# Loads issued earlier, exponentials ahead of the choice, score rows moved: a change of order in an attention and mixture-of-depths kernel

## The chip, the cores and the metric

One core of a Trainium2 chip runs the kernel. The metric is the device time of one execution in microseconds, as the median of the runs shown. The core has a matrix engine (TensorE, PE, whose weight loads are listed as PEld), a vector engine (VectorE, DVE), a scalar engine (ScalarE, ACT), GpSimd (POOL) and a sync engine (SyncE, SP), which here only issues DMAs. The engines run side by side; each one runs its own instructions in program order and waits on semaphores for the others.

## The reference

Efficient attention on 8 batches of 8 heads, 576 tokens and a head size of 64, followed by a mixture-of-depths block that sends 128 tokens of each batch through an MLP:

```python
q_s = softmax(q, axis=-1); k_s = softmax(k, axis=2)          # float32
kv = np.einsum('bhsd,bhse->bhde', k_s, v)
x = np.einsum('bhsd,bhde->bhse', q_s, kv)                    # to (B, S, H*D), H*D = 512
scores = np.einsum('bsd,d->bs', x, w_gate)
out = x.copy()
for b in range(B):
    top_idx = np.argpartition(-scores[b], capacity)[:capacity]     # capacity = 128
    xe = x[b, top_idx]
    ye = np.maximum(xe @ w1, 0.0) @ w2                             # 512 -> 1024 -> 512
    g = 1.0 / (1.0 + np.exp(-scores[b, top_idx]))
    out[b, top_idx] = xe + g[:, None] * ye
```

## The kernel before

A unit is one batch with four of its eight heads (`NU` = 16 units; unit u is batch u // 2, and `qd` = u % 2 says which four heads). Its 576 tokens are 512 main tokens, four to a partition, and 64 last ones; the last tokens of q, k and v are loaded for all eight heads at once with the unit whose `qd` is 0. `load(u, ...)` issues these loads on the sync queue: 0.52 MB for each of q, k and v, and 0.13 MB for each set of last rows, in pieces of 256 bytes. The pool `ld` has three buffers for each of q, k and v, so load(u) waits until unit u - 3 has been used up.

For each unit `prepare(u)` takes the exponentials of q and k on ACT (`q_exp`, `k_exp`; with `qd` = 0 those of the last rows too) and copies v on DVE next to a column of ones (`v_copy`). `kv_mm` makes the product of k's exponentials and v on PE, and `kv_out` turns it into a block-diagonal right-hand side (`kv_diag`) on ACT and DVE. `q_t` transposes q's exponentials on PE and scales them on the way out on ACT; `q_t_last` does the same for the last tokens, with DVE. `x_mm` makes the attention output in PSUM, `x_out` normalizes it on DVE and stores it with a DMA on the sync queue (0.52 MB per unit, and 0.13 MB for a batch's last tokens).

After the second unit of a batch `score` sums the gate scores on DVE, `score_last` folds the last tokens' scores with a small matmul (L325), and `score_row` transposes the scores to a row on PE, copied out by ACT. `compare` (DVE) compares every score with every other, `count` (PE, L370, copied out by ACT) adds the results to ranks, and `pick` (DVE, then ACT and POOL) finds the tokens with the chosen ranks: its gate is `g`, an ACT instruction, and it gathers the chosen rows from the output in DRAM with an indirect DMA on POOL (L388), which so needs the stores of that batch. `turn` transposes the gathered rows on PE (L404), `mlp1` and `mlp2` are the two MLP products in eight pieces each (L418, L428), and `finish` adds the result and scatters it back with POOL.

The order is written out by hand (`tc.manual_schedule()`): every engine, and the sync queue, gets its instructions in the order of the program text. One pass of the loop is a slot s. In slot s PE does kv_mm and the transposes of unit s + 1 and x_mm of unit s, while exponentials and copies are prepared for unit s + 2. In even slots from 2 on the batch (s - 2) // 2 is chosen (`compare`, `count`, `pick`); in odd slots the batch s // 2 gets its scores. From slot 4 on (`LAG`) the MLP of batch (s - 4) // 2 runs between these steps, mlp1 in the even slot and mlp2 in the odd one; `pieces(n)` puts n of the eight pieces there. `turn` stands at the head of the even slot.

Before the change prepare(s + 2) stands behind `pick`, and load(s + 3) at the end of the slot, behind the stores of x_out. The weights w1 and w2 (2.10 MB each) are loaded at the end of slots 0 and 1.

Of the kernel before, what the change touches and what calls it, by code (L numbers as in the profile page):

```python
# [8 lines left out]
F32 = mybir.dt.float32  # L9
# [8 lines left out]
def kernel(  # L18
# [20 lines left out]
    nc = tc.nc  # L39
    B, H, S, D = q.shape  # L40
    DM, F = moe_w1.shape
    P = 128
    R = 4
    MAIN = R * P
    REM = S - MAIN
    KD = DM // P
    KF = F // P
    SD = S * D
# [1 line left out]
    C = D + 2  # L50
    NG = 18
    LOW = 2.0 ** -30
    WARM = 12
    assert S == MAIN + 64 and D == 64 and DM == H * D and DM == 512 and H % 4 == 0
    assert 1 < capacity < S and KF == 8 and NQ == 2
    HALF = S // 2
# [5 lines left out]
    const = ctx.enter_context(tc.tile_pool(name="const", bufs=1))  # L62
    ld = ctx.enter_context(tc.tile_pool(name="ld", bufs=3))
# [6 lines left out]
    def bank(tag, bufs):  # L70
        return ps.tile([P, 512], F32, tag=tag, name=tag, bufs=bufs)

    def part(i):
        return slice(64 * i, 64 * i + 64)

    units = [(b, qd) for b in range(B) for qd in range(NQ)]
    NU = len(units)
# [3 lines left out]
    raw = {}  # L81

    def load(u, which):
        b, qd = units[u]
        for what in which:
            src = {"q": q, "k": k, "v": v}[what]
            t = ld.tile([P, 4, R, D], F32, tag=what, name=what)
            nc.sync.dma_start(  # L88
                out=t.rearrange("p h r d -> p h (r d)"),
                in_=bass.AP(tensor=src.tensor, offset=src[b, 4 * qd].offset,  # L90
                            ap=[[R * D, P], [SD, 4], [1, R * D]]))
            raw[what, u] = t
            if qd == 0:
                t = ld.tile([REM, H, D], F32, tag=what + "_l", name=what + "_l", bufs=2)
                nc.sync.dma_start(
                    out=t, in_=bass.AP(tensor=src.tensor, offset=src[b, 0].offset + MAIN * D,
                                       ap=[[D, REM], [SD, H], [1, D]]))
                raw[what + "l", b] = t

    load(0, "qkv")  # L100
    load(1, "qkv")
# [3 lines left out]
    ones_b = const.tile([P, 4 * P], BF16, name="ones_b")  # L105
    nc.vector.memset(ones_b, 1.0)
    warm = const.tile([P, 1], F32, name="warm")
    nc.scalar.activation(out=warm, in_=ones_b[:, :1], func=AF.Exp)
    for _ in range(2):
        w_ps = bank("tp", 2)  # L110
        for _ in range(WARM // 2):
            nc.tensor.matmul(out=w_ps, lhsT=ones_b[:, :P], rhs=ones_b, start=True, stop=True)
    wgm = const.tile([P, NQ, 2, 2, D], F32, name="wgm")
    nc.sync.dma_start(out=wgm.rearrange("p a i h d -> p (a i h d)"),
                      in_=bass.AP(tensor=moe_w_gate.tensor, offset=moe_w_gate.offset,
                                  ap=[[0, P], [1, DM]]))
    w1 = const.tile([P, KD, F], F32, name="w1")
    w2 = const.tile([P, KF, DM], F32, name="w2")
# [7 lines left out]
    for n in range(2):  # L126
        t = const.tile([P, 4, R, D + 1], F32, name=f"v_ones{n}")
# [3 lines left out]
        t = const.tile([P, H, D + 1], F32, name=f"v_last{n}")  # L131
# [3 lines left out]
        t = const.tile([P, H, D], F32, name=f"k_last{n}")  # L135
        nc.gpsimd.memset(t[part(1)], 0.0)
        k_last.append(t)
        t = const.tile([P, 2, 2, C], F32, name=f"kv_diag{n}")
# [23 lines left out]
    def late_constants():  # L162
        nc.vector.tensor_add(fold, ident[:, :REM], ident[:, REM:])
        nc.vector.tensor_scalar(after, col_minus_p, 0.0, None, op0=OP.is_gt)
        for h in range(2):
            nc.vector.memset(wgm[part(h), :, :, 1 - h], 0.0)
# [8 lines left out]
    def k_exp(u):  # L175
        b, qd = units[u]
        ke = at.tile([P, 2, R, 2, D], F32, tag="ke", name="ke")
        kr = by_row(raw.pop(("k", u)))
        for i in range(2):
            nc.scalar.activation(out=ke[:, i], in_=kr[:, i], func=AF.Exp)  # L180
        st["ke", u] = ke
        if qd == 0:
            nc.scalar.activation(out=k_last[b % 2][part(0)], in_=raw.pop(("kl", b)), func=AF.Exp)

    def q_exp(u):
        b, qd = units[u]
        qe = at.tile([P, 2, R, 2, D], F32, tag="qe", name="qe")
        qr = by_row(raw.pop(("q", u)))
        for i in range(2):
            nc.scalar.activation(out=qe[:, i], in_=qr[:, i], func=AF.Exp)  # L190
        st["qe", u] = qe
        if qd == 0:
            ql = at.tile([REM, H, D], F32, tag="ql", name="ql")
            nc.scalar.activation(out=ql, in_=raw.pop(("ql", b)), func=AF.Exp)
            st["ql", b] = ql
# [116 lines left out]
    def score(b):  # L312
        s = md.tile([P, R + 2], F32, tag="s", name="s")
        a = md.tile([P, NG], F32, tag="s_a", name="s_a")
        nc.vector.tensor_add(a, sr[b][:, 0], sr[b][:, 1])
        a3 = a.rearrange("p (n m) -> p n m", n=3)
        nc.vector.reduce_sum(out=s[:, 0:3], in_=a3[:, :, 0:4], axis=AX.X)
        nc.vector.reduce_sum(out=s[:, 3:4], in_=a3[:, 1:3, 4:6], axis=AX.XY)
        nc.vector.reduce_sum(out=s[:, 5:6], in_=a3[:, 0, 4:6], axis=AX.X)
        st["s", b] = s  # L320

    def score_last(b):
        s = st["s", b]
        f_ps = bank("mm", 2)
        nc.tensor.matmul(out=f_ps[:REM, :1], lhsT=fold, rhs=s[:, 5:6], start=True, stop=True)  # L325
        nc.vector.tensor_copy(out=s[:REM, 4:5], in_=f_ps[:REM, :1])

    def score_row(b):
        s = st["s", b]
        srow = md.tile([P, S], F32, tag="srow", name="srow")  # L330
        t_ps = bank("tp", 2)
        for r in range(R):
            nc.tensor.transpose(out=t_ps[:, r * P:(r + 1) * P], in_=s[:, r:r + 1].to_broadcast([P, P]),  # L333
                                identity=ident)
        nc.scalar.copy(out=srow[:, :MAIN], in_=t_ps)  # L335
        l_ps = bank("tp", 2)
        nc.tensor.transpose(out=l_ps[:, :REM], in_=s[:REM, 4:5].to_broadcast([REM, P]),
                            identity=ident[:REM, :REM])
        nc.scalar.copy(out=srow[:, MAIN:], in_=l_ps[:, :REM])
        st["srow", b] = srow  # L340
# [183 lines left out]
    def prepare(u):  # L524
        q_exp(u)
        k_exp(u)
        v_copy(u)

    LAG = 4

    with tc.manual_schedule():
        prepare(0)
        late_constants()
        kv_mm(0)
        kv_out(0)
        q_t(0, 0)
        q_t(0, 1)
        q_t_last(0)
        load(2, "qkv")
        prepare(1)  # L540

        number = None
        for s in range(NU + LAG):

            mlp_b, odd = divmod(s - LAG, 2)
            busy = s >= LAG
            first = busy and odd == 0
            piece = mlp1 if first else mlp2
            f_next = 0

            def pieces(n):
                nonlocal f_next
                for _ in range(n if busy else 0):
                    each(piece, mlp_b, f_next)
                    f_next += 1

            ends = s // 2 if s % 2 == 1 and s < NU else None
            chosen = (s - 2) // 2 if s % 2 == 0 and 2 <= s <= NU else None
            if first:
                each(turn, mlp_b)  # L560
            if s + 1 < NU:
                kv_mm(s + 1)
                kv_out(s + 1)
                pieces(1)
                q_t(s + 1, 0)
                q_t(s + 1, 1)
            else:
                pieces(1)
            if s == NU - 1:
                x_mm(s)  # L570
                x_out(s)
                score(ends)
            if chosen is not None:
                compare(chosen)
            pieces(2)
            if s + 1 < NU:
                q_t_last(s + 1)
            if s < NU - 1:
                x_mm(s)
                x_out(s)  # L580
                if ends is not None:
                    score(ends)
            pieces(2)
            if chosen is not None:
                count(chosen)
                pick(chosen)
            if ends is not None:
                score_last(ends)
            if s + 2 < NU:
                prepare(s + 2)  # L590
            pieces(2)
            if ends is not None:
                score_row(ends)
            pieces(1)
            if busy and odd == 1:
                each(finish, mlp_b)
            if s == 0:
                nc.sync.dma_start(out=w1, in_=moe_w1.rearrange("(d p) f -> p d f", p=P))
            if s == 1:
                nc.sync.dma_start(out=w2, in_=moe_w2.rearrange("(f p) d -> p f d", p=P))  # L600
            if s + 3 < NU:
                load(s + 3, "qkv")
            if s == NU:
                number = sums_in_range()

# [27 lines left out]
```

## Time and profile before

| | us |
|---|---|
| median of 3 runs | 307.67 (307.02 to 307.70) |
| profiled execution, its own time | 306.83 |
| its span, first to last instruction | 305.0 |

| engine | busy us | share of the span | instructions |
|---|---|---|---|
| PE | 257.1 | 84% | 1669 |
| PE weight loads | 199.7 | 65% | 1669 |
| DVE | 120.8 | 40% | 452 |
| ACT | 99.4 | 33% | 210 |
| POOL | 21.0 | 7% | 32 |

The busy times come from one profiled execution. Weight loads overlap with matmuls. Each f32 matmul is recorded as two instructions. The mean granted clock of PE is 0.943 of 2.4 GHz; it changes between two levels in the course of the run. A row of the timeline gives the start, the busy time, the engine, the line, the operation with its tiles and, in brackets, how long the engine was idle before it and who released it.

### The profile page before, as it was taken

To read this page: it belongs to the slowest core of one execution; us is meant where nothing else is said; L and a number is where in the kernel's file an instruction comes from. 1 tells how busy PE (TensorE), PEld (TensorE's weight loads), DVE (VectorE), ACT (ScalarE), POOL (GpSimd) and SP (SyncE) were. 2 spreads that over 40 slices of the span, in tenths; PEclk is the share of its full clock that TensorE was granted. 3 is DMA by queue.
4 is the path that set the end of the run, shared out by engine and by line. 5 is a ranking of instruction groups with operands and counts; after the bars stand their busy time and mean duration, and the time that the engine had idled before them with its cause. 6 is when DMAs were issued, how large, how long until landed. Compare 5 with 4: busy or idle time off the path is not lost.

```text
span 305.0 us, 4416 instructions
## 1 busy us (share of the span) xinstructions
PE 257.1 (84%) x1669; PEld 199.7 (65%) x1669; DVE 120.8 (40%) x452; ACT 99.4 (33%) x210; POOL 21.0 (7%) x32
## 2 busy tenths in 40 slices
PE   6467737576997999799979998999979999998991
PEld 2456617475986588757967597749855887583850
DVE  1122332915463426332831465146524465351000
ACT  4256222245316331542265124703272411120100
POOL 5000000010001010101010001001010101101101
PEclk9679976959899999999999999999999999999997
DMA  7990799981946195808690586349552121201100
GB/s 186 296 262 12 243 373 378 218 273 65 234 134 224 38 236 145 276 0 220 161 290 21 168 213 204 108 100 256 148 189 72 50 69 34 89 34 37 38 6 37
DMA packets 51789, 46.77 MB, mean 153 GB/s; under 512 B 14256, under 2 KB 49072, under 8 KB 51760
## 3 DMA queue, kind: packets, MB, share of 16 engines
q1 hardware_dynamic: 50480, 42.21, 49.4%
q0 software_dynamic: 1280, 4.20, 3.9%
q8 instruction: 15, 0.25, 0.3%
q14 instruction: 14, 0.11, 0.1%
HBM read 34.87 MB, written 11.53 MB: 152 GB/s over the span
## 4 chain that ended last, share of the span: by engine, by line
PE 67%; DVE 11%; ACT 7%; DMA 6%; issue 3%; SPq 3%; POOL 0%; POOLq 0%; ACTq 0%
PE mm L428 16%; PE mm L418 14%; PE kv L212 11%; PE x L273 9%; PE tp L370 4%; DMA v<-in_v_dram 4%; PE tp L243 3%; PE kv L215 3%; DMA wgm<-in_moe_w_gate_dram 3%; DVE xs L292 3%; DVE junk_p L383 2%; SPq L88 2%; PE x L276 2%; ACT qe L190 2%; PE mm L404 1%
## 5 line engine op out<-in xcount | busy, mean ns | idle before, releaser
L418 PE MATMUL mm<-xT,w 128*128 128x128 f32 x512 | 63.1, 278 | 1.4 <-ACT xT L406 1.4
L212 PE MATMUL kv<-v_ones,ke 128*128 128x130 f32 x256 | 42.6, 318 | 25.3 <-ACT ke L180 14.0
L428 PE MATMUL mm<-w,hT 128*128 128x512 f32 x128 | 62.0, 608 | 0.0
L418 PEld LDWEIGHTS mm<-xT,w 128*128 128x128 f32 x512 | 59.2, 192 | 4.0 <-ACT xT L406 1.9
L212 PEld LDWEIGHTS kv<-v_ones,ke 128*128 128x128 f32 x256 | 38.6, 229 | 27.9 <-ACT ke L180 15.3
L428 PEld LDWEIGHTS mm<-w,hT 128*128 128x128 f32 x128 | 21.8, 189 | 17.4 <-issue 16.9
L273 PE MATMUL x<-kv_diag,qT 128*128 128x132 f32 x256 | 33.0, 282 | 0.0
L273 PEld LDWEIGHTS x<-kv_diag,qT 128*128 128x128 f32 x256 | 30.0, 190 | 1.5 <-issue 0.5
L227 ACT COPY kv_diag<-kv 64x130 f32<-64x130 f32 x32 | 8.4, 263 | 46.1 <-DVE krec L224 45.6
L421 ACT ACTIVATE hT<-mm 128x512 f32<-128x512 f32 x16 | 9.4, 590 | 39.9 <-PE mm L418 39.9
L245 ACT ACTIVATE qT<-tp,krec 128x512 f32<-128x512 f32 x32 | 20.3, 684 | 6.3 <-PE tp L243 6.2
L224 DVE RECIPROCAL krec<-kv 128x2 f32<-128x2 f32 x16 | 2.7, 170 | 48.9 <-PE kv L215 48.9
L436 DVE SCALAR_TENSOR_TENSOR o<-mm,g,xr 128x512 f32<-128x512 f32 x8 | 6.0, 750 | 39.2 <-PE mm L428 39.2
L190 ACT ACTIVATE qe<-q 128x512 f32<-128x512 f32 x32 | 18.3, 621 | 9.1 <-DMA q<-in_q_dram 9.1
L388 POOL DMA_INDIRECT xr<-out_dram,idx x8 | 9.0, 1131 | 161.9 <-PE mm L418 75.7
L335 ACT COPY srow<-tp 128x512 f32<-128x512 f32 x8 | 4.7, 584 | 44.8 <-PE tp L333 44.8
L180 ACT ACTIVATE ke<-k 128x512 f32<-128x512 f32 x32 | 18.2, 618 | 1.5 <-DMA k<-in_k_dram 1.5
L243 PEld LDWEIGHTS tp<-ident,qe 128*128 128x128 f32 x128 | 16.3, 152 | 2.6 <-issue 1.4
L243 PE MATMUL tp<-ident,qe 128*128 128x128 f32 x128 | 17.9, 286 | 0.0
L348 DVE TENSOR_SCALAR less<-srow,s 128x128 bf16<-128x128 f32 (+4 forms) x40 | 16.2, 405 | 0.0
L437 POOL DMA_INDIRECT out_dram<-o,idx x8 | 8.0, 1002 | 116.6 <-DVE o L436 106.1
L199 DVE COPY v_ones<-v 128x1024 f32<-128x1024 f32 x16 | 10.9, 680 | 13.0 <-DMA v<-in_v_dram 13.0
(80 smaller groups left out, 251.2 us busy)
## 6 DMA issues: line engine op xcount, KB each, us to landing
q<-in_q_dram SPq DMA_DIRECT2D x16, 512.0 KB
k<-in_k_dram SPq DMA_DIRECT2D x16, 512.0 KB
v<-in_v_dram SPq DMA_DIRECT2D x16, 512.0 KB
out_dram<-xs SPq DMA_DIRECT2D x16, 512.0 KB
w<-in_moe_w_dram SPq DMA_DIRECT2D x2, 2048.0 KB
q_l<-in_q_dram SPq DMA_DIRECT2D x8, 128.0 KB
k_l<-in_k_dram SPq DMA_DIRECT2D x8, 128.0 KB
v_l<-in_v_dram SPq DMA_DIRECT2D x8, 128.0 KB
```

The source lines that it names most:

```text
L180: nc.scalar.activation(out=ke[:, i], in_=kr[:, i], func=AF.Exp)
L190: nc.scalar.activation(out=qe[:, i], in_=qr[:, i], func=AF.Exp)
L199: nc.vector.tensor_copy(out=v_ones[u % 2][:, :, :, :D], in_=raw.pop(("v", u)))
L212: nc.tensor.matmul(out=kv[:, i], lhsT=ke[:, i, r].rearrange("p h d -> p (h d)"), rhs=vo[:, pair, r], start=(r == 0), stop=False)
L243: nc.tensor.transpose(out=t_ps[:, r * P:(r + 1) * P], in_=qe[:, i, r].rearrange("p h d -> p (h d)"), identity=ident)
L245: nc.scalar.activation(out=st["qT", u][:, i].rearrange("p r c -> p (r c)"), in_=t_ps, func=AF.Copy, scale=krec[:, u, i:i + 1])
L273: nc.tensor.matmul(out=x[:, r, i] if r < 3 else x[:, 1 + i, 2], lhsT=qT[:, i, r], rhs=kd[:, i], start=True, stop=True)
L348: nc.vector.tensor_scalar(less[rows, j, :cols.stop], srow[rows, :cols.stop], own, None, op0=OP.is_lt)
L370: nc.tensor.matmul(out=r_ps[:, a:z], lhsT=ones_b[rows, :P], rhs=rhs, start=(n == 0), stop=(n == len(todo) - 1), skip_group_check=True)
L418: nc.tensor.matmul(out=h_ps[:, f % 4 * m:(f % 4 + 1) * m], lhsT=w1[:, d, f * P:(f + 1) * P], rhs=xT[:, d, :m], start=(d == 0), stop=(d == ...
L421: nc.scalar.activation(out=hT[:, f - 3:f + 1, :m], in_=h_ps[:, :4 * m].rearrange("p (f c) -> p f c", f=4), func=AF.Relu)
L428: nc.tensor.matmul(out=st["y", b, n][:m], lhsT=st["hT", b, n][:, f, :m], rhs=w2[:, f], start=(f == 0), stop=(f == KF - 1))
```

## The change

The warm-up matmuls at the start get another form: 12 bf16 matmuls over 512 columns become 40 small f32 ones. `load` issues the last rows behind the main loads of all three tensors. load(2) and load(3) are issued behind prepare(0), w1 and load(4) behind prepare(1), and load(s + 5) in the slot, behind prepare(s + 2) and ahead of the stores of x_out; w2 in slot 0. prepare(s + 2) stands ahead of `compare`. In odd slots `score_last` stands two pieces later and `score_row` behind the eighth piece. In slot 15 x_mm stands at the head of the slot, ahead of all pieces.

```diff
@@ load
-            if qd == 0:
-                t = ld.tile([REM, H, D], F32, tag=what + "_l", name=what + "_l", bufs=2)
...
+        for what in which if qd == 0 else "":
+            src = {"q": q, "k": k, "v": v}[what]
+            t = ld.tile([REM, H, D], F32, tag=what + "_l", name=what + "_l", bufs=2)
...
@@ warm-up (WARM = 12 becomes 10)
-    for _ in range(2):
-        w_ps = bank("tp", 2)
-        for _ in range(WARM // 2):
-            nc.tensor.matmul(out=w_ps, lhsT=ones_b[:, :P], rhs=ones_b, start=True, stop=True)
+    ones_f = const.tile([P, P], F32, name="ones_f")
+    nc.vector.memset(ones_f, 1.0)
+    w_ps = [bank("tp", 2), bank("tp", 2)]
+    for n in range(2 * WARM):
+        c = part(n % 2)
+        nc.tensor.matmul(out=w_ps[0][c, 66 * (n // 2 % 4):66 * (n // 2 % 4) + 65], lhsT=ones_f[:, :64],
+                         rhs=ones_f[:, :65], start=True, stop=True)
+    for n in range(2 * WARM):
+        c = part(n % 2)
+        nc.tensor.matmul(out=w_ps[n % 2][:, 66 * (n // 2 % 4):66 * (n // 2 % 4) + 66], lhsT=ones_f[c],
+                         rhs=ones_f[c, :66], start=True, stop=True)
@@ ahead of the loop
+    def load_weights(n):
...
         prepare(0)
+        load(2, "qkv")
+        load(3, "qkv")
         late_constants()
...
         q_t_last(0)
-        load(2, "qkv")
         prepare(1)
+        load_weights(0)
+        load(4, "qkv")
@@ the slot
+            last = s == NU - 1
...
-            else:
+            elif not last:
                 pieces(1)
-            if s == NU - 1:
+            if last:
                 x_mm(s)
                 x_out(s)
                 score(ends)
+                pieces(3)
+                score_last(ends)
+                pieces(1)
+                score_row(ends)
+            if s + 2 < NU:
+                prepare(s + 2)
             if chosen is not None:
                 compare(chosen)
             pieces(2)
             if s + 1 < NU:
                 q_t_last(s + 1)
-            if s < NU - 1:
+            if s + 5 < NU:
+                load(s + 5, "qkv")
+            if s == 0:
+                load_weights(1)
+            if s < NU and not last:
                 x_mm(s)
                 x_out(s)
                 if ends is not None:
                     score(ends)
-            pieces(2)
+            if not last:
+                pieces(2)
             if chosen is not None:
                 count(chosen)
                 pick(chosen)
-            if ends is not None:
+            pieces(2)
+            if ends is not None and not last:
                 score_last(ends)
-            if s + 2 < NU:
-                prepare(s + 2)
-            pieces(2)
-            if ends is not None:
+                pieces(1)
                 score_row(ends)
-            pieces(1)
+            elif not last:
+                pieces(1)
             if busy and odd == 1:
                 each(finish, mlp_b)
-            if s == 0:
-                nc.sync.dma_start(out=w1, in_=moe_w1.rearrange("(d p) f -> p d f", p=P))
-            if s == 1:
-                nc.sync.dma_start(out=w2, in_=moe_w2.rearrange("(f p) d -> p f d", p=P))
-            if s + 3 < NU:
-                load(s + 3, "qkv")
```

## Rows read from the trace of the kernel before

**Rows 1.** The page's first part: busy us (share of the span) xinstructions of each engine.
```profile
PE 257.1 (84%) x1669; PEld 199.7 (65%) x1669; DVE 120.8 (40%) x452; ACT 99.4 (33%) x210; POOL 21.0 (7%) x32
```

**Rows 2.** Stretches: length, busy us of PE, PEld, DVE, ACT, POOL, PE clock, DMA share, GB/s.
```profile
75.39:94.28 18.89, 17.36 (x136) 15.94 (x135) 9.75 (x36) 6.72 (x16) 0.99 (x1) 0.91 0.80 215
94.28:126.45 32.17, 30.04 (x208) 23.31 (x208) 14.61 (x54) 12.14 (x27) 2.19 (x2) 1.00 0.59 165
```

**Rows 3.** Timeline of PE, slots 5 and 13: kv_mm and score_last with idle time before.
```profile
94.28 1.16 PE L212 MATMUL kv<-v_ones,ke 128*128 128x130 f32 x8 [1.53 <-ACT ke L180]
...
105.52 0.28 PE L325 MATMUL mm<-s,fold 128*64 128x1 f32 x2 [0.60 <-DVE s L319]
...
222.98 1.16 PE L212 MATMUL kv<-v_ones,ke 128*128 128x130 f32 x8 [1.53 <-ACT ke L180]
...
234.23 0.28 PE L325 MATMUL mm<-s,fold 128*64 128x1 f32 x2 [0.60 <-DVE s L319]
```

**Rows 4.** Timeline of ACT and DVE at the end of slot 6.
```profile
124.11 0.20 ACT L392 ACTIVATE g<-sel 128x1 f32<-128x1 f32 x1 [1.63 <-DVE junk_p L383]
124.22 1.13 ACT L190 ACTIVATE qe<-q 128x512 f32<-128x512 f32 x2
...
124.62 0.68 DVE L199 COPY v_ones<-v 128x1024 f32<-128x1024 f32 x1
...
125.21 0.41 DVE L201 COPY v_last<-v_l 64x512 f32<-64x512 f32 x1
...
125.78 1.13 ACT L180 ACTIVATE ke<-k 128x512 f32<-128x512 f32 x2
```

**Rows 5.** Timeline of slot 6: compare's last instruction, count's first, pick's first.
```profile
117.30 0.28 DVE L353 SCALAR_TENSOR_TENSOR ties<-srow,s,after 64x64 bf16<-64x64 f32 x1
...
120.08 0.29 PE L370 MATMUL tp<-less,ones_b 128*128 128x288 bf16 x1
...
122.52 0.82 DVE L383 SCALAR_TENSOR_TENSOR junk_p<-rank,slot_no,tok_row 128x576 bf16<-128x576 f32 x1 [2.33 <-ACT rank L372]
```

**Rows 6.** Timeline of PE in slot 5, behind x_mm.
```profile
102.56 0.45 PE L276 MATMUL x<-kv_diag,qTl 128*64 128x132 f32 x4
...
102.94 1.98 PE L428 MATMUL mm<-w,hT 128*128 128x512 f32 x4
```

**Rows 7.** Stretches ahead of slot 4; the last two columns are DMA share, GB/s.
```profile
2.00:23.50 21.50, 13.54 (x53) 9.81 (x52) 3.76 (x17) 7.55 (x16) 2.62 (x8) 0.78 1.07 267
23.50:32.00 8.50, 5.19 (x41) 4.51 (x40) 3.69 (x14) 4.90 (x10) 0.00 (x0) 0.96 0.01 3
32.00:68.00 36.00, 23.32 (x147) 20.72 (x148) 14.26 (x55) 10.80 (x24) 1.27 (x1) 0.77 1.03 314
```

**Rows 8.** The gather of batch 0 in POOL's timeline, and all gathers' times to landing.
```profile
60.78 1.27 POOL L388 DMA_INDIRECT xr<-out_dram,idx  x1 [55.98 <-DMA v_l<-in_v_dram]
...
DMA to landing us min/median/max: 3.3/4.6/6.9
```

**Rows 9.** Timeline of PE: kv_mm of units 2, 3 and 4.
```profile
32.04 1.13 PE L212 MATMUL kv<-v_ones,ke 128*128 128x130 f32 x8 [2.67 <-DVE v_ones L199]
...
46.81 2.07 PE L212 MATMUL kv<-v_ones,ke 128*128 128x130 f32 x8 [3.75 <-DVE v_ones L199]
...
62.79 2.10 PE L212 MATMUL kv<-v_ones,ke 128*128 128x130 f32 x8 [4.57 <-ACT ke L180]
```

**Rows 10.** Stretches at half clock: after kv_mm(4) starts, and in slot 4.
```profile
62.80:68.20 5.40, 5.40 (x25) 5.40 (x26) 0.17 (x1) 1.32 (x4) 0.00 (x0) 0.50 0.87 296
75.80:78.30 2.50, 2.50 (x14) 2.50 (x13) 0.00 (x0) 0.78 (x3) 0.00 (x0) 0.50 0.68 164
```

**Rows 11.** Timeline of the start: warm-up, kv_mm(0), and the mask of w_gate.
```profile
1.47 5.30 PE L112 MATMUL tp<-ones_b 128*128 128x512 bf16 x12 [1.47 <-DVE side L124]
...
11.68 2.07 PE L212 MATMUL kv<-v_ones,ke 128*128 128x130 f32 x8 [4.91 <-DVE v_ones L199]
...
16.84 0.64 DVE L166 MEMSET wgm<- 64x256 f32 x2 [4.44 <-DMA wgm<-in_moe_w_gate_dram]
```

More of the change, by code (lines that the diff above doesn't have):

```diff
@@ L52 @@
     LOW = 2.0 ** -30
-    WARM = 12
+    WARM = 10
     assert S == MAIN + 64 and D == 64 and DM == H * D and DM == 512 and H % 4 == 0
@@ L92, in load @@
             raw[what, u] = t
-            if qd == 0:
-                t = ld.tile([REM, H, D], F32, tag=what + "_l", name=what + "_l", bufs=2)
[L95 to L98, printed above, removed]
+        for what in which if qd == 0 else "":
+            src = {"q": q, "k": k, "v": v}[what]
+            t = ld.tile([REM, H, D], F32, tag=what + "_l", name=what + "_l", bufs=2)
+            nc.sync.dma_start(
+                out=t, in_=bass.AP(tensor=src.tensor, offset=src[b, 0].offset + MAIN * D,
+                                   ap=[[D, REM], [SD, H], [1, D]]))
+            raw[what + "l", b] = t
     load(0, "qkv")
@@ L529 @@
     LAG = 4
+    def load_weights(n):
+        if n == 0:
+            nc.sync.dma_start(out=w1, in_=moe_w1.rearrange("(d p) f -> p d f", p=P))
+        else:
+            nc.sync.dma_start(out=w2, in_=moe_w2.rearrange("(f p) d -> p f d", p=P))
     with tc.manual_schedule():
         prepare(0)
+        load(2, "qkv")
+        load(3, "qkv")
         late_constants()
```

## The prediction

> **What bounds the kernel now.** I read the busy shares first: TensorE (PE) is busy for 257.1 of 305.0 us, DVE, ACT and POOL for 40, 33 and 7% of the span [rows 1]. So the time is PE work plus PE's idle time, and the question is where the 48 us of idle lie. The table by stretches comes next. From slot 5 on the kernel repeats with a period of two slots: kv_mm(6) starts at 94.28 and kv_mm(14) at 222.98, four pairs later [rows 3], so a pair takes 128.70 / 4 = 32.18 us. PE is busy for 30.04 of them at full clock [rows 2]; 2.13 us are idle. The timeline of PE names them: 1.53 us ahead of kv_mm in each odd slot, released by the exponentials of k, and 0.60 us ahead of the little matmul of score_last, released by DVE [rows 3]. There are five of each, at 94.28 to 222.98 and at 105.52 to 234.23. The rest of the idle time lies ahead of 75.39 us, where slot 4 begins with turn(0), and in the tail. Ahead of 75.39 PE waits 2.67, 3.75 and 4.57 us for its inputs at kv_mm(2), kv_mm(3) and kv_mm(4) [rows 9], and the DMA engines stand still from 23.5 to 32 us though loads are left [rows 7]: load(3) stands on the sync queue behind the store of unit 0 and w1.
>
> **Exponentials ahead of the choice.** In the even slot ACT does g, then qe, ql, ke in program order. g waits for the choice, so qe starts only 0.11 us after it, at 124.22, and the first ke at 125.78; kv_mm starts 0.67 us after that [rows 4]. In the changed order prepare(s+2) stands ahead of compare, when ACT has done with qT, and nothing it needs comes from the choice. The inputs have landed long before, since load runs five units ahead. kv_mm then follows the last mlp1 piece. Gain: 5 x 1.53 = 7.65 us. What is late next? On DVE the two v copies of prepare (0.68 and 0.41 us, overlapping by 0.09, so about 1.0 us) now stand ahead of compare [rows 4]. Behind compare are queued qTl, x_out and pick. The compare ends at 117.58 and count starts at 120.08 [rows 5], 2.5 us of cover, so 1.0 us more costs nothing; the choice of pick itself waits 2.33 us for the rank [rows 5], which covers x_out's delay. x_mm(s) reads the qTl of unit s, written a slot earlier, so the late qTl of unit s+1 holds nothing up. Without that cover the price would be 1.0 us in each of the slots 4, 6, 8, 10 and 12, 5 us in all. I take 0.
>
> **Score rows later.** In an odd slot with MLP work score_last now stands behind four mlp2 pieces rather than two after x_mm. x_mm's last matmuls start at 102.56, the four matmuls of two pieces last from 102.94 to 104.92, and the score matmul starts at 105.52 [rows 3, 6]. Two more pieces are about 1.7 us, against 0.60 us of waiting. Gain 5 x 0.60 = 3.0 us. score_row now stands next to the head of the next slot; its ACT copies come ahead of xT's, but kv_mm (over 2 us) runs between turn and the first mlp1 piece, which hides them. In slots 1 and 3 there are no pieces, so the wait there stays.
>
> **Loads earlier.** load(3) needs only prepare(0), the inputs of kv_mm(0), which starts at 11.68 [rows 11], and w1 needs nothing, so the DMA hole at 23.5 to 32 is filled, and the three early waits (10.99 us together) go: slots 0 to 3 alone would let turn(0) run at 75.39 - 10.99 = 64.4. But two loads and both weights now stand ahead of the stores on the same queue. turn(0) needs the gather of batch 0, and that needs the stores of units 0 and 1. By program order the sync queue sends, after the load of unit 2 (done by 23.5 [rows 7]): units 3 (1.57 MB), w1 (2.10), unit 4 with its last rows (1.97), unit 5 (1.57), w2 (2.10), store 0 (0.52), unit 6 (1.97), store 1 (0.66): 12.45 MB. In the two loaded stretches the DMA moved 267 GB/s with 0.79 of 5.77 MB (13.6%) in 256-byte pieces (the last rows), and 314 GB/s with 0.39 of 11.3 MB (3.5%) in them [rows 7]. The new list has 0.79 of 12.45 MB (6.3%), so an estimate between the two rows is 301 GB/s, 41.4 us, and store 1 lands at 64.9. The gather took 3.3 to 6.9 us from issue to landing, the longest the one at 60.78 with loads in flight [rows 8]; unit 7's load is in flight here too, so 6.9. turn(0) then starts at 71.8, not 64.4: the gather is late next, and the gain is 75.39 - 71.8 = 3.6 us.
>
> Only one wait of this kind, PE's at turn(0), is new. After it PE comes from several us of idleness. After the 4.57 us of idleness ahead of 62.79 the granted clock was 0.50 (1.2 GHz) for 5.40 us of solid work, against 2.50 us from 75.80 to 78.30 at the present start of slot 4 [rows 9, 10]. At half clock half the time is lost, so this costs (5.40 - 2.50) / 2 = 1.45 us more than now. Start: 3.6 - 1.45 = 2.1 us.
>
> On the order of the queue, no row of before shows a store that waits behind several loads. The Trainium skill says, in "DMA: Bandwidth & Descriptors", section "Queues, rings and completion order", that each DMA engine takes a queue's descriptors in ring order, though a later one may finish its write earlier; that rule speaks against putting loads ahead of stores. By it the sum stands at 71.8; without it the first rival below comes out.
>
> **Warm-up.** 12 matmuls (5.30 us [rows 11]) go; 40 small f32 ones come, which the trace would count as 80, as the 128 matmuls of L212 show (x8 for 4). Eight such instructions with 130 columns took 1.16 us at full and 2.07 us at half clock [rows 3, 9]. With 65 or 66 columns 80 of them cost between half of the first (5.8 us) and all of the second (20.7 us); I take 11.6. They end near 13 us, and kv_mm(0) begins there instead. It is hidden: kv_out(0) waits for wgm, which released it at 16.84 [rows 11], at an unchanged place in the queue. If the bound of 20.7 holds, kv_mm(0) ends some 6 us late, and the 64.4 becomes about 70, still ahead of 71.8. So 0, bound from 0 to 6 us of cover used.
>
> **Last product first.** In slot 15 x_mm(15) runs ahead of the pieces; PE was busy there in either order, and score_last stands behind three pieces (2.6 us) where it needs about 2.5. 0, within 0.7 us either way. The tail after it is the same work.
>
> **The sum.** 7.65 + 3.0 + 2.1 = 12.75 us. The profiled execution took 306.83 us (span 305.0 and 1.83 around it): 294.1. The median of the three runs is 307.67, 0.84 above it, so 294.9 for a median.
>
> **Rivals.** (a) *The stores are not held up.* If the DMA engines let the two stores pass early, or move the list faster, the gather is off the path and slot 4 starts at 64.4, where PE's own chain lets it: 7.4 us earlier, 287.5. For it: the DMA reached more than the mean in stretches; against it: 12.45 MB would have to go in 34 us (366 GB/s), above both rows. The Trainium skill's "DMA: Bandwidth & Descriptors", section "Specifications", gives about 358 GB/s as HBM's limit for a core; by this figure an estimate is 34.8 us for the list, slot 4 at 65.2 and 288.3. The two rows (267 and 314) don't bear that rate out as a mean.
> (b) *The DMA is as slow as in the first stretch.* At 267 GB/s the list takes 46.6 us, turn(0) runs at 77.0, 1.6 us later than now, and with the 1.45 us of clock the start loses 3.1: 307.67 - 10.65 + 3.1 = 300.1. For it: half of the loaded units carry last rows; against it: the weights go in large pieces.
> (c) *Slower than before*, by the same place: the gather of batch 0 behind the loads. It decides once turn(0) comes later than 71.8 + 12.75 = 84.5, which needs the list to move at 12.45 / (84.5 - 6.9 - 23.5) = 230 GB/s or less; at 200 GB/s turn(0) is at 92.6, 8.1 us past that point, and the time 307.67 + 8.1 = 315.8. Both loaded rows are above 230.
> (d) *The waits of the pairs don't go*: the exponentials start earlier but kv_mm then waits for something else, the v copies behind kv_out, say. Then the start and the score waits are left: 307.67 - 2.1 - 3.0 = 302.6. Against it: DVE is idle for half of the pair [rows 2].
>
> **How the numbers follow.** The forecast has 0.50, (a) 0.20, (b) 0.17, (d) 0.07, (c) 0.03, and 0.03 is left for others. The range takes in (a) and (b), 287.0 to 300.1; outside it are (c), (d) and parts of (a). A difference of 0.3% (0.9 us) is what a measurement of this kernel can tell from no change; all cases but (c) are faster by more: 0.95 faster, 0.02 within, 0.03 slower.
>
> **What would show it.** Exponentials: no wait of L212 for ACT from slot 5 on, the pair at 30.0 to 30.1 us instead of 32.18. Score: no wait of L325 from slot 5 on. Start: DMA without a hole from 2 to about 65 us, PE idle ahead of the first L404 with the gather as its releaser, and half clock after it. Wrong would be: a pair over 31 us (a new wait on DVE or ACT), or slot 4 before 66 or after 76 us.

## The result and the profile after

| | before | after |
|---|---|---|
| median us | 307.43 | 289.81 |
| profiled span us | 305.0 | 288.0 |
| kv_mm(6) starts (slot 5) | 94.28 | 88.92 |
| a pair of slots | 32.18 | 29.52 |
| turn(0) starts | 75.39 | 70.81 |

The ratio is 0.942 (95% interval 0.939 to 0.945): 17.6 us less for the medians, 17.0 for the two spans. Forecast were 294.9, and 12.75 us.

The stretches of the changed kernel, with the columns of [rows 2]: slot 4, and the first two pairs.

```profile
70.81:88.92 18.11, 18.11 (x134) 16.87 (x135) 9.58 (x35) 7.09 (x15) 0.33 (x1) 0.85 0.81 215
88.92:118.44 29.52, 29.52 (x209) 23.17 (x208) 14.53 (x54) 12.25 (x26) 1.61 (x2) 1.00 0.61 179
118.44:147.96 29.52, 29.52 (x209) 23.17 (x208) 14.53 (x54) 12.25 (x26) 1.96 (x2) 1.00 0.60 177
```

In these stretches PE has no idle time: busy equals the length, where [rows 2] had 2.13 us less in a pair. The busy time itself fell too, from 30.04 to 29.52. PE's timeline of the changed kernel (to be read against [rows 3, 6]):

```profile
70.81 1.11 PE L412 MATMUL mm<-ident,xr 128*128 128x128 f32 x4 [6.66 <-DMA xr<-out_dram,idx]
...
88.92 1.06 PE L220 MATMUL kv<-v_ones,ke 128*128 128x130 f32 x8
...
97.34 3.70 PE L436 MATMUL mm<-w,hT 128*128 128x512 f32 x8
100.97 0.28 PE L333 MATMUL mm<-s,fold 128*64 128x1 f32 x2
```

kv_mm and the score matmul have no bracket any more: nothing is waited for. The one long wait left stands ahead of turn(0), 6.66 us for the gather. The choice in slot 6, with the v copies ahead of it (compare [rows 5]):

```profile
107.26 0.69 DVE L207 COPY v_ones<-v 128x1024 f32<-128x1024 f32 x1
...
107.87 0.41 DVE L209 COPY v_last<-v_l 64x512 f32<-64x512 f32 x1
...
111.91 0.27 DVE L361 SCALAR_TENSOR_TENSOR ties<-srow,s,after 64x64 bf16<-64x64 f32 x1
...
113.77 0.29 PE L378 MATMUL tp<-less,ones_b 128*128 128x288 bf16 x1
```

compare ends at 112.18, count starts at 113.77: the cover shrank from 2.50 to 1.59 us, by 0.91, and holds.

The DMA's part: the stretch from 23.5 us to the gather's start and 5 us of it, the store of the second unit's last tokens on the sync queue, and the gather on POOL.

```profile
23.50:63.60 40.10, 30.99 (x218) 26.62 (x216) 21.42 (x85) 19.23 (x41) 0.00 (x0) 0.88 1.08 320
27.00:32.00 5.00, 5.00 (x43) 4.60 (x43) 2.64 (x8) 3.33 (x7) 0.00 (x0) 1.00 1.03 405
```

```profile
57.02 2.52 SPq L312 DMA_DIRECT2D out_dram<-xl  x2
```

```profile
63.66 1.12 POOL L396 DMA_INDIRECT xr<-out_dram,idx  x1 [58.88 <-DVE s L334]
```

The hole of [rows 7] is gone: 320 GB/s from 23.5 to 63.6 us, and 405 in a stretch of 5 us, above the 358 at which the prediction also worked out rival (a). The gather starts at 63.66 and lands 7.1 us later, ahead of turn(0) at 70.81. The profile names a DVE copy of slot 3 as its releaser; the runs below show that the gather waited for the store instead: it moves with the bytes ahead of the store, and the second profiled run of the same kernel names the store.

### The profile page after: what moved, and what is told of

It reads as the page before. It is cut to its first block, busy times and chain, and to the rows that moved or that the text cites. A ratio compares the mean times of both kernels' runs of the same rounds, so it can differ in the third digit from the quotient of the medians.

```text
span 288.0 us, 4554 instructions
## 1 busy us (share of the span) xinstructions
PE 255.4 (89%) x1737; PEld 202.7 (70%) x1737; DVE 120.0 (42%) x453; ACT 99.7 (35%) x210; POOL 19.8 (7%) x32
## 4 chain that ended last, share of the span: by engine, by line
PE 79%; DVE 6%; DMA 5%; ACT 3%; SPq 3%; issue 1%; POOL 0%; POOLq 0%; ACTq 0%
PE mm L436 20%; PE mm L426 20%; PE kv L220 11%; PE x L281 10%; PE tp L378 4%; PE tp L251 3%; PE kv L223 3%; DMA wgm<-in_moe_w_gate_dram 3%; DMA xr<-out_dram,idx 2%; PE x L284 2%; SPq L88 2%; PE mm L412 2%; PE tp L265 1%; PE tp L341 1%; ACT qT L253 1%
## 5 line engine op out<-in xcount | busy, mean ns | idle before, releaser
L436 PE MATMUL mm<-w,hT 128*128 128x512 f32 x128 | 60.5, 604 | 0.0
L220 PE MATMUL kv<-v_ones,ke 128*128 128x130 f32 x256 | 41.6, 314 | 3.6 <-ACT ke L188 3.6
L220 PEld LDWEIGHTS kv<-v_ones,ke 128*128 128x128 f32 x256 | 38.0, 226 | 4.5 <-ACT ke L188 4.2
L396 POOL DMA_INDIRECT xr<-out_dram,idx x8 | 7.9, 987 | 162.3 <-PE mm L426 79.6
L251 PEld LDWEIGHTS tp<-ident,qe 128*128 128x128 f32 x128 | 15.0, 144 | 2.6 <-issue 2.6
L251 PE MATMUL tp<-ident,qe 128*128 128x128 f32 x128 | 16.8, 274 | 0.0
L378 PE MATMUL tp<-less,ones_b 128*128 128x288 bf16 (+1 forms) x80 | 15.7, 288 | 0.9 <-DVE less L356 0.8
L300 DVE TENSOR_TENSOR xs<-x,qrec 128x768 f32<-128x768 f32 x16 | 15.3, 957 | 0.5
```

The costliest lines, as they stand in the source:

```text
L220: nc.tensor.matmul(out=kv[:, i], lhsT=ke[:, i, r].rearrange("p h d -> p (h d)"), rhs=vo[:, pair, r], start=(r == 0), stop=False)
L251: nc.tensor.transpose(out=t_ps[:, r * P:(r + 1) * P], in_=qe[:, i, r].rearrange("p h d -> p (h d)"), identity=ident)
L300: nc.vector.tensor_mul(xs[b][:, 0:3, qd], heads[:, :, 0:4, :D], rec[:, :, 0:4].to_broadcast([P, 3, 4, D]))
L378: nc.tensor.matmul(out=r_ps[:, a:z], lhsT=ones_b[rows, :P], rhs=rhs, start=(n == 0), stop=(n == len(todo) - 1), skip_group_check=True)
L436: nc.tensor.matmul(out=st["y", b, n][:m], lhsT=st["hT", b, n][:, f, :m], rhs=w2[:, f], start=(f == 0), stop=(f == KF - 1))
```

## The experiments

My theory was: PE bounds the pairs, and the waits in them come from program order; the start is bound by the gather of batch 0, and that by the bytes that stand ahead of a store on the sync queue. Where no ratio or median is given, a variant was executed once. The kernel before, executed beside the variants, mostly had spans between 302 and 308 us, so a difference of 2 us in one span says little by itself; there the rows of the trace carry the argument.

**The exponentials alone.** The kernel before with one step moved:

```diff
+            if s + 2 < NU:
+                prepare(s + 2)
             if chosen is not None:
                 compare(chosen)
...
-            if s + 2 < NU:
-                prepare(s + 2)
```

> The kernel before with prepare(s + 2) ahead of compare and nothing else changed. Theory (the pair is bound by PE, and the 1.53 us ahead of kv_mm, with 0.16 us of drain ahead of it and 0.24 us of slow restart behind it, go with the order of ACT's program): a late pair takes 32.18 - 1.93 = 30.25 us and no kv_mm waits for an exponential there. Early the loads are too late for this order: in slot 2 DVE stands at the v copy of unit 4, which landed at 61.2 in the kernel before, with compare(0) queued behind it, so kv_mm(4) comes at about 67.4 instead of 62.8 and turn(0) near 80; slot 4 loses some 3 us more in the same way. So early some 4.5 to 7.5 us are lost and later some 9 are won: a span of 300 to 304. Rival (the pairs' gain comes from the early loads, not from the order of the exponentials): pairs stay at 32.2, and the span is 309 to 313.

Measured: a span of 319.2 us, 14.2 more than before and outside both expectations. DVE at slot 2, then PE early, and in a late pair (turns at 155.47 and 187.81):

```profile
67.27 0.69 DVE L199 COPY v_ones<-v 128x1024 f32<-128x1024 f32 x1 [10.22 <-DMA v<-in_v_dram]
```

```profile
49.70 0.37 PE L325 MATMUL mm<-s,fold 128*64 128x1 f32 x2 [12.12 <-DVE s L319]
...
68.91 0.42 PE L370 MATMUL tp<-less,ones_b 128*128 128x288 bf16 x1 [9.12 <-DVE less L350]
```

```profile
166.31 0.29 PE L370 MATMUL tp<-less,ones_b 128*128 128x288 bf16 x1
...
167.45 0.28 PE L370 MATMUL tp<-less,ones_b 128*128 128x288 bf16 x1 [0.22 <-DVE less L348]
...
168.31 0.92 PE L370 MATMUL tp<-less,ones_b 64*128 64x288 bf16 x4 [0.57 <-DVE less L348]
...
169.63 2.94 PE L418 MATMUL mm<-xT,w 128*128 128x128 f32 x24
...
184.09 0.28 PE L325 MATMUL mm<-s,fold 128*64 128x1 f32 x2 [1.27 <-DVE s L319]
```

kv_mm waits for no exponential in the pairs, as the theory had it, but the late pair from turn to turn takes 32.34 us, not 30.25. The v copy, now ahead of the other DVE work, waits for its load 14 of 16 times, and what is queued behind it on DVE (compare, x_out, score) hands the delay to PE. The matmuls of count wait for compare chunk by chunk and take 3.32 us (166.31 to 169.63) instead of 1.90 (120.08 to 121.98 in slot 6 of before), and the score matmul waits 1.27 us instead of 0.60: 1.42 and 0.67 us, together the 2.09 between 30.25 and 32.34. Early the delay feeds itself: the copy waits for a load, x_out waits behind the copy, the store waits for x_out, and the next load stands behind the store. I had expected the loss in slots 2 and 4 (4.5 to 7.5 us) but not in slot 1 (12.12 us, of which before had 2.51). Up to turn(0) PE has 10.0 us more idle time than before and 2.8 us more busy time, at a mean granted clock of 0.75 rather than 0.82.

**The score rows alone.** The kernel before with:

```diff
-            if ends is not None:
+            if ends is not None and last:
                 score_last(ends)
             if s + 2 < NU:
                 prepare(s + 2)
             pieces(2)
-            if ends is not None:
+            if ends is not None and not last:
+                score_last(ends)
+            if ends is not None and last:
                 score_row(ends)
             pieces(1)
+            if ends is not None and not last:
+                score_row(ends)
```

> The kernel before with score_last two pieces later and score_row behind the eighth piece, in all odd slots but the last. Theory (PE-bound pair; the wait of 0.60 us goes, and 0.12 us more, because the transposes of score_row and turn now stand next to each other and PE changes once less between the two forms): a pair takes 31.46 us, five odd slots give 3.6 us, span 301.4. Rival (only the wait goes): 31.58 us, span 302.0. If score_row next to turn delays turn's copy or the compare, the pair stays at 32.2.

Measured: span 301.4, median 304.17, ratio 0.990 (0.986 to 0.995), a difference under 2%. PE in two successive odd slots:

```profile
94.33 1.16 PE L212 MATMUL kv<-v_ones,ke 128*128 128x130 f32 x8 [1.53 <-ACT ke L180]
...
125.79 1.16 PE L212 MATMUL kv<-v_ones,ke 128*128 128x130 f32 x8 [1.53 <-ACT ke L180]
```

The pair is 31.46 us: 0.72 less than 32.18, the wait of 0.60 and 0.12 more, the size that the theory had.

**The loads alone.** The kernel before with load(2) and load(3) behind prepare(0), w1 and load(4) behind prepare(1), and in the slot, behind pick:

```diff
             if s + 2 < NU:
                 prepare(s + 2)
+            if s + 5 < NU:
+                load(s + 5, "qkv")
+            if s == 0:
+                load_weights(1)
...
-            if s + 3 < NU:
-                load(s + 3, "qkv")
```

> The kernel before with load(2), load(3) behind prepare(0), w1 and load(4) behind prepare(1), w2 and load(s + 5) behind prepare(s + 2), which stays behind pick; so the stores of a slot go ahead of its loads. Theory (turn(0) waits for the gather, which waits for the stores behind the loads): here the stores of units 0 and 1 stand behind 7.86 MB less 0 loads of unit 6, about 10.5 MB after 23.5 us, so they land near 57 us, the gather is no longer last, and turn(0) comes when PE is ready, 65 to 68 us; the pairs stay at 32.18 us; span 295 to 298. Rival (the gather waits for something in slot 3 and not for the stores): turn(0) at 70 us or later, span 300 or more.

Measured: span 302.9, 2.1 us less than before, which is within the spread of before; expected were 295 to 298. PE's kv_mm of units 2 and 4 and turn(0), then the gather:

```profile
32.02 1.55 PE L218 MATMUL kv<-v_ones,ke 128*128 128x130 f32 x8 [2.67 <-DVE v_ones L205]
...
60.64 2.10 PE L218 MATMUL kv<-v_ones,ke 128*128 128x130 f32 x8 [4.57 <-ACT ke L186]
...
73.24 0.88 PE L410 MATMUL mm<-ident,xr 128*128 128x128 f32 x4
```

```profile
58.63 1.12 POOL L394 DMA_INDIRECT xr<-out_dram,idx  x1 [53.83 <-DVE idx L392]
```

The gather is not late here: idx released it, and turn(0) has no wait. But of the three early waits of [rows 9] only the 3.75 us of kv_mm(3) went. The 2.67 and 4.57 us stayed to the hundredth: v_copy stands behind x_out, and the exponentials behind pick. These two never came from the DMA. The rival's figures came out (turn(0) after 70, a span over 300), but for this reason and not for the rival's. Of PE's time up to turn(0) 4.1 us of idle went, and 1.9 us of busy time came, at a mean granted clock of 0.79 rather than 0.82.

**The warm-up of before in the changed kernel.**

```diff
-    for n in range(2 * WARM):
-        c = part(n % 2)
...
+    for _ in range(2):
+        w_ps = bank("tp", 2)
+        for _ in range(WARM // 2):
+            nc.tensor.matmul(out=w_ps, lhsT=ones_b[:, :P], rhs=ones_b, start=True, stop=True)
```

> The changed kernel with the 12 bf16 warm-up matmuls of before. Theory (the start is hidden behind the DMA list and the gather): turn(0) at 70.8 within 0.5 us, span 288.0 within 0.9. Rival (the warm-up holds PE's clock up and saves time at the start that lasts): turn(0) 1 to 2 us later, span 289 to 290.

Measured: span 287.1, median 289.45, ratio 0.943 (0.937 to 0.950), the same as the changed kernel's. Its gather and turn(0):

```profile
63.08 1.13 POOL L389 DMA_INDIRECT xr<-out_dram,idx  x1 [58.28 <-DMA out_dram<-xl]
```

```profile
70.20 1.11 PE L405 MATMUL mm<-ident,xr 128*128 128x128 f32 x4 [10.40 <-DMA xr<-out_dram,idx]
```

The warm-up changes nothing that lasts. PE was ready 4 us earlier here (it waits 10.40 us rather than 6.66), and turn(0) came only 0.6 us earlier: the gather sets it. The 4 us are not the old warm-up's doing, since the changed kernel had them too in its second profiled run, shown further down. And here the profile names the store of the last tokens as the gather's releaser.

**The stores ahead of the loads.** The changed kernel with:

```diff
-            if s + 5 < NU:
-                load(s + 5, "qkv")
             if s == 0:
-                load_weights(1)
+                load(s + 5, "qkv")
             if s < NU and not last:
                 x_mm(s)
                 x_out(s)
                 if ends is not None:
                     score(ends)
+            if 1 <= s and s + 5 < NU:
+                load(s + 5, "qkv")
+            if s == 1:
+                load_weights(1)
```

> The changed kernel with load(s + 5) of the slots from 1 on, and w2, issued behind the stores of the slot (w2 in slot 1). Theory (turn(0) waits for the gather of batch 0, the gather for the store of unit 1, and that for 12.45 MB in the queue's order): ahead of that store stand 8.4 MB now, it lands near 51 us, the gather starts when pick(0) is done, at 55 to 56, and turn(0) comes when PE is ready, at 64 instead of 70.8; up to 1.3 us of half clock go too. The pairs stay at 29.52 us. Span 280 to 281.5. Rival (the gather waits for the score copy of slot 3, which the profile names as its releaser): the gather starts at 63 us as now, span 287 to 288.

Measured: span 274.7, median 277.85, ratio 0.908 (0.892 to 0.925). The gather, turn(0), and the stretch behind it:

```profile
52.09 1.13 POOL L396 DMA_INDIRECT xr<-out_dram,idx  x1 [47.29 <-DVE idx L394]
```

```profile
60.08 0.66 PE L412 MATMUL mm<-ident,xr 128*128 128x128 f32 x4
```

```profile
60.00:80.00 20.00, 20.00 (x166) 17.99 (x167) 10.78 (x42) 9.46 (x21) 0.96 (x1) 1.00 1.06 326
```

The gather starts 11.6 us earlier, at once after idx, and turn(0) has no wait. The gain over the changed kernel is 13.3 us of span where 6.5 to 8 were expected: PE came to turn(0) at 60.08 rather than 64, since the granted clock stayed at full speed through slots 1 to 3 in this run, and with no idleness ahead of turn(0) slot 4 ran at full clock too. Part of this is the luck of the start: against the second profiled run of the changed kernel, whose start also ran at full clock (span 286.7, PE ready at 59.7), the gain is 12.0 us, 9.8 at turn(0) and 2.2 in slot 4.

**w2 alone later**, from slot 0 to behind the stores of slot 1, in the changed kernel:

```diff
-            if s == 0:
-                load_weights(1)
...
                 if ends is not None:
                     score(ends)
+            if s == 1:
+                load_weights(1)
```

> The changed kernel with w2 alone moved, from slot 0 to behind the stores of slot 1. Theory (bytes ahead of the store of unit 1): 2.10 MB less, at 300 to 400 GB/s 5 to 7 us, so that the gather starts at 57 to 58.5 and lands at 64 to 65.5; turn(0) at 64 to 65.5, span 281 to 283. Rival (the gather waits for slot 3's score copy): start of the gather at 63, span 287 to 288.

Measured: span 281.1; gather and turn(0):

```profile
57.35 1.12 POOL L396 DMA_INDIRECT xr<-out_dram,idx  x1 [52.56 <-DVE kv_diag L241]
```

```profile
64.19 1.11 PE L412 MATMUL mm<-ident,xr 128*128 128x128 f32 x4 [0.50 <-DMA xr<-out_dram,idx]
```

With 2.10 MB less ahead of the store the gather starts 6.31 us earlier and turn(0) 6.62 us. That is the theory's figure; the score copy of slot 3 comes only at 62 us here, so it does not release the gather.

**Twice more of the v copies.** In the changed kernel, ahead of the v copy in the even slots 4 to 12:

```diff
+                if chosen is not None and busy:
+                    for _ in range(2):
+                        v_again(s + 2)
                 v_copy(s + 2)
```

> The changed kernel with the two copies of v made three times, ahead of compare, in the even slots 4 to 12: 2.0 us more of DVE's time in front of each of five choices. Theory (compare has cover: it now ends at 112.18 and count starts at 113.77, and count reads its last chunk later): 0 to 0.5 us per slot, the pair at 29.5 to 30.0, span 288 to 290.5. Rival (the copies in front of compare come at their price): 2.0 us per slot, the pair at 31.5, span 298.

Measured: span 288.2, and in successive odd slots:

```profile
118.59 1.06 PE L225 MATMUL kv<-v_ones,ke 128*128 128x130 f32 x8
...
148.11 1.06 PE L225 MATMUL kv<-v_ones,ke 128*128 128x130 f32 x8
```

The pair is 29.52 us, unchanged with 2.0 us more on DVE ahead of each compare. In slot 6 compare now ends at 114.22, 0.30 us behind the start of count at 113.92, and count takes no longer for it. The cover is real, and a little more than the 1.59 us read off the first matmul of count, since count's matmuls wait chunk by chunk.

**Slot 15 as before**, in the changed kernel:

```diff
-            elif not last:
+            else:
                 pieces(1)
             if last:
                 x_mm(s)
                 x_out(s)
                 score(ends)
-                pieces(3)
+                pieces(4)
                 score_last(ends)
-                pieces(1)
+                pieces(2)
                 score_row(ends)
+                pieces(1)
...
-            pieces(2)
+            if not last:
+                pieces(2)
```

> The changed kernel with the order of before in slot 15 (one piece, x_mm, four pieces, score_last, two pieces, score_row, the last piece). Theory (PE is busy there in either order): slot 15 takes the same 10.5 us, span 288.0 within 0.5. Rival (the product at the head lets the choice of the last batch start earlier and shortens the tail): 1 us or more longer, 289 to 290.

Measured: span 286.8, 1.2 us below the changed kernel, and below the expected bound of 0.5. The slot itself did not do it. turn(0) came at 69.87 (0.94 us earlier, from a start that ran at full clock), and slot 4 was shorter by 0.2 us. From the end of slot 14's last piece to the turn of slot 16, both orders take 10.47 us.

**The exponentials behind pick again**, in the version with the stores first, and load(s + 5) behind them:

```diff
-            if s + 2 < NU:
-                prepare(s + 2)
             if chosen is not None:
                 compare(chosen)
...
                 pick(chosen)
+            if s + 2 < NU:
+                prepare(s + 2)
+            if s + 5 < NU:
+                load(s + 5, "qkv")
+            if s == 1:
+                load_weights(1)
```

> The version with the stores first, with prepare(s + 2) put back behind pick, and load(s + 5) behind it. Everything else of the change stays. Theory (the order of the exponentials and copies is worth much only when the loads are early, and the early loads only with that order): the pair is 29.52 + 1.53 + 0.16 + 0.24 = 31.45 us, kv_mm(2) and kv_mm(4) wait 2.67 and 4.57 us again, turn(0) comes at about 73 as in the run with early loads alone, and the span is that run's 302.9 less five score waits of 0.72: 299.3, so that the order alone is worth 24.6 us here. Rival (the parts add up: exponentials 7.65 and no more): 274.7 + 7.7 = 282.4.

Measured: span 297.7, 23.0 us more than with the exponentials ahead.

```profile
59.14 2.10 PE L220 MATMUL kv<-v_ones,ke 128*128 128x130 f32 x8 [4.57 <-ACT ke L188]
...
71.93 1.11 PE L412 MATMUL mm<-ident,xr 128*128 128x128 f32 x4
...
90.57 1.16 PE L220 MATMUL kv<-v_ones,ke 128*128 128x130 f32 x8 [1.53 <-ACT ke L188]
...
122.03 1.16 PE L220 MATMUL kv<-v_ones,ke 128*128 128x130 f32 x8 [1.53 <-ACT ke L188]
```

The pair is 31.46 us, against 29.52: 1.94 us, where 1.93 were expected, and both early waits are back. turn(0) moves from 60.08 to 71.93. PE up to turn(0), here and in the version with the stores first (columns of [rows 2]):

```profile
0.00:71.93 71.93, 49.62 (x340) 44.74 (x341) 26.73 (x108) 28.20 (x58) 5.00 (x17) 0.85 1.00 290
```

```profile
0.00:60.08 60.08, 42.27 (x341) 37.34 (x341) 26.39 (x108) 28.01 (x58) 5.02 (x17) 0.97 1.08 295
```

Of the 11.85 us, 4.50 are idle time of PE and 7.35 the same work at a lower granted clock (0.85 against 0.97). As the start of one program runs at either clock, one run of each can't tell how much of the 7.35 belongs to the order. Behind turn(0) slot 4 is 3.07 us longer and four pairs 7.76. So the order of the exponentials costs 14.2 us where the loads are late and gives about 23 where they are early, a part of it the clock's, while the early loads alone give 2.1. That the order is worth much more with early loads is shown; the size of 23.0 comes from one pair of runs, in which load(s + 5) moved along.

**The changed kernel and the version with the stores first once more, on one chip.**

> The changed kernel once more, beside the version with the stores first on one chip. Theory: median 288.5 to 290, the gather of batch 0 the releaser of the first L412.

> The version with the stores first once more, for its time beside the changed kernel's. Theory: 11 to 13 us below the changed kernel, 276 to 279, ratio to the kernel before 0.90 to 0.91, turn(0) at 60 to 64 without a wait for the gather.

Measured: the changed kernel has a ratio of 0.939 (0.934 to 0.944) to the kernel before and a median of 289.36 us; the version with the stores first has 0.908 (0.904 to 0.912) and 279.19. Before took 308.1 us here, so the stores are worth 0.031 x 308.1 = 9.5 us by the ratios and 10.2 by the medians of all executions, under the expected 11 to 13. In this run of the changed kernel turn(0) again waits for the gather, and the gather for the store:

```profile
62.69 1.12 POOL L396 DMA_INDIRECT xr<-out_dram,idx  x1 [57.89 <-DMA out_dram<-xl]
```

```profile
69.88 1.11 PE L412 MATMUL mm<-ident,xr 128*128 128x128 f32 x4 [10.23 <-DMA xr<-out_dram,idx]
```

In the profiled run of the other version turn(0) starts at 59.74 without a wait. That version beats both kernels.

## Why the prediction was right, and where its terms were off

The three mechanisms were the ones forecast, and the new wait too. The spans differ by 17.0 us: 5.36 up to kv_mm(6), 128.70 - 118.08 = 10.62 in four pairs, 1.02 behind them. The terms:

| term | forecast | measured |
|---|---|---|
| exponentials, five slots | 7.65 | 9.65 |
| score rows, five slots | 3.0 | 3.6 |
| turn(0) | 3.6 | 4.6 |
| half clock behind turn(0) | -1.45 | -0.9 |
| warm-up, slot 15 | 0 | 0 |
| sum | 12.75 | 17.0 |

**Exponentials: right place, undersized.** The forecast took only the idle 1.53 us per slot, and so a pair of 30.0 to 30.1 us (29.52 measured). The order gives 0.40 us more. PE in slots 5 and 6 of before, then after:

```profile
96.76 1.02 PE L428 MATMUL mm<-w,hT 128*128 128x512 f32 x2
...
121.98 2.94 PE L418 MATMUL mm<-xT,w 128*128 128x128 f32 x24
126.45 1.16 PE L212 MATMUL kv<-v_ones,ke 128*128 128x130 f32 x8 [1.53 <-ACT ke L180]
```

```profile
91.16 1.02 PE L436 MATMUL mm<-w,hT 128*128 128x512 f32 x2
...
115.66 2.94 PE L426 MATMUL mm<-xT,w 128*128 128x128 f32 x24
118.44 1.06 PE L220 MATMUL kv<-v_ones,ke 128*128 128x130 f32 x8
```

From the start of the last three mlp1 pieces to kv_mm it was 4.47 us and is 2.78: 1.69, so 0.16 over the wait, the last matmul's end that now overlaps the next. And kv_mm to the first mlp2 piece took 2.48 us in slot 5 (from 94.28) and takes 2.24 (from 88.92): its first matmuls came slowly behind the wait (1.16 us for eight in [rows 3], 1.06 after), and so did the first two with k_last. The run without the order showed the whole, 1.94 us a pair.

**Score rows: right, 0.12 us a slot short.** The run with that edit alone gave the same 0.72. The likely reason, which no run isolates: score_row now stands next to turn, so that PE goes once less from transposes back to mlp2.

**DVE's cover: right.** 1.0 us more ahead of compare cost nothing, nor did 3.0.

**turn(0): right in kind.** The gather is what is late next. The list moved in 40.1 us, where 41.4 were worked out, if the gather started as the last store landed, and the gather took 7.1 us against 6.9. The runs with w2 later (6.3 us for 2.10 MB) and with the stores first show that bytes ahead of the store set it. The Trainium skill's rule ("DMA: Bandwidth & Descriptors", section "Queues, rings and completion order") is that a DMA engine takes a queue's descriptors in ring order, and the runs agree with it: taking 2.10 MB from ahead of the store brought the gather 6.31 us forward. Rival (a), slot 4 at 64.4, did not come true because of this; it is what w2 later gives (64.19). Rival (b), the DMA at 267 GB/s, is out with 320, (c) with turn(0) ahead of 84.5, and (d) with kv_mm's wait gone. That PE itself came to turn(0) at 64.1, where 64.4 were worked out, is luck: the 64.4 carries over the half clock in the start of before, and in the second profiled run PE was there at 59.7.

**Half clock: right in kind, oversized.** I counted 2.50 us of half clock for the present slot 4, the solid part of it; turn(0) itself ran at half clock there too, so the difference was 0.9 rather than 1.45. This is slot 4's length, 18.89 before and 18.11 after, with the 1.69 us of wait and drain taken off the first.

**What failed is an attribution that the sum did not need.** I put all three early waits to the loads ("the three early waits (10.99 us together) go"). The run with the loads alone kept two of them, 7.24 us, which come from the order of prepare. I also treated the exponentials and the loads as separate terms, with the early loads as a remark ("the inputs have landed long before"). They are not separate: the order is worth -14.2 us without the loads. The forecast was for both together, so its sum did not suffer. Its three gains all came out larger than forecast (by 2.0, 0.6 and 1.0 us) and the price of half clock smaller (by 0.55), so the misses add up, to about 4.2 us, instead of cancelling.

## What to carry to other kernels

An engine that works in program order and takes up a load early turns a late load into a delay of everything behind it. So moving the consumer up and issuing the load earlier are one edit, not two; each alone can be worth little or less than nothing (here 2.1 us gained and 14.2 lost). When loads are pulled ahead on a queue that also carries stores, look for a reader of the stores: here a gather of the output, for which PE stood still for 7 to 10 us until the stores went first again. And a wait of the matrix engine can cost more than it shows (here 1.93 us for 1.53 of idle time), since the drain ahead of it and the slow start behind it are booked as busy.

## What was not expected of the hardware

The start of one and the same program runs at either level of the clock. In the profiled run of the changed kernel shown above the granted clock fell to 0.50 (1.2 GHz) ahead of slot 2, at about 39 us, behind a wait of 2.52 us, and PE reached turn(0)'s wait at 64.1 us; in its second profiled run the clock stayed at 1.00 (2.4 GHz) behind a wait of the same length, and PE reached it at 59.7, as in the run with the old warm-up and that with the old slot 15. In the changed kernel this hides behind the gather (turn(0) at 70.81 and 69.88). In the version with the stores first nothing hides it. Its six times in the last experiment run from 276.3 us (mean granted clock 0.990) to 282.0 (0.954), with 278.5 at 0.966 and 279.3 at 0.979 between them. Only the first has a trace, so that the spread comes from the start is not shown, and time and clock go together only roughly.

The 80 small warm-up instructions took 6.9 us (1.61 to 8.51), near the lower of the bounds, 5.8 and 20.7, and not the 11.6 that the prediction took.
